# Keys and values one token to a partition, a bias table of single distances, key tiles in the order 0, 3, 1, 2

## The chip, the cores and the metric

The kernel runs on one core of a Trainium2 chip. The metric is the device time of one execution in microseconds, taken as the median of several runs.

## The reference

Attention with a T5-style relative position bias, followed by a mixture of low-rank adapters over the concatenated heads. Batch 8, 8 heads, 576 tokens, head dimension 64; 32 buckets of distance; 8 adapters of rank 16, of which each token uses two.

```python
scores = scale * np.matmul(q, k.transpose(0, 1, 3, 2))        # (8, 8, 576, 576)
n = np.abs(pos[:, None] - pos[None, :])
bucket = np.where(n < 16, n, min(16 + int(log-ratio * 15), 31))   # 31 from n = 128 on
scores = scores + bias_table[bucket].transpose(2, 0, 1)[None]
attn = softmax(scores)
x = (attn @ v), heads side by side                               # (4608, 512)
logits = x @ w_gate                                               # 8 adapters
out = x + sum over the two largest logits of w * ((x @ A[e]) @ B[e])
```

The bias of a query and a key depends on their distance alone, and all distances from 128 on share one bucket. Softmax does not change when that bucket's value is taken off everywhere, so only the band of distances below 128 needs a bias.

## The kernel before, in words

The work is cut into 32 units: one batch and one pair of heads (`units`, 8 x 4). A unit's 576 tokens are 512 "main" tokens and a tail of 64. The tails of all heads of a batch are loaded and cast together (`load_tail`, `cast_tail`).

**Loads.** `load` (L102 to L113) issues the DMAs of a unit's q, k and v from the SP queue: one DMA of 256 KB for q (L112) and, for k and for v, one of 128 KB for each head (L109). Only the two DMAs of the first unit's k are issued from ScalarE's queue. q puts four consecutive tokens on a partition (runs of 1 KB in DRAM). k and v are in two halves of 256 tokens, two consecutive tokens on a partition (runs of 512 B). So key tile c = 2g + e holds the tokens 256 g + 2 p + e. The staging tiles (`qs`, `ks`, `vs`) have four buffers; the program of unit u issues the loads of unit u + 4. SP also stores the results (`out_dram<-ot`, L310, L332), in program order among the loads.

**Casts and turns.** `cast` copies a staged tile to bf16: q and k at L139, v at L135, on GpSimd in the steady state. In the program of unit u, `prep(u)` casts q and k of unit u + 2, and in some units those of unit u + 3 as well; `prep_late(u)` casts v of unit u + 1. `turn` transposes q and k of unit u + 2 on TensorE (L379), together with tiles of the adapters' part, and VectorE copies the result out of PSUM (L381).

**Scores.** `keys(u, c)` computes a 128 x 512 score tile of both heads. Each has four matmuls of 64 x 64 (`QUADS`: two heads and two halves f of 64 keys). First the scores (L436), 512 columns each; then the bias (L441), which adds a piece of the table `Wt` through the anti-diagonal matrix `anti`, only in the band near the diagonal. `BAND` gives for each half where the band starts, its width n in places and its offset in the table; a place covers the four queries of a partition. Of the widths 64, 96, 96, 64, four times each is streamed: 256 or 384 columns. One exponential on ScalarE (L445) then covers 128 x 1024. The key tiles of a unit are taken in the order `KO`; three of them, then the output steps of the unit before, then the fourth. For the last two units `keys_half` (L454, L461, L465) does the same with tiles split by queries.

**Edges.** `edges(u)` computes the scores between main and tail tokens (L495, L498) and their exponential (L500). Their bias is a factor on the exponentials: `edge_l` on GpSimd (L505, table `EL`) for the tail's keys, `edge_t` on VectorE (L510, table `ET`) for the tail's queries. `corner_scores` does the tail against itself, with the factor `EC`.

**The bias table.** Eight heads' distances are laid out in `gx`, from it the even and odd distances in `gp`; `gp` is written to DRAM (L665) and read back as 64 shifted rows a head (`table`, L208) into `Wt`. `near_rows` takes the exponential of the part near the diagonal (L204, tile `Wn`), and `factors_l` and `factors_t` make `EL`, `EC` and `ET` of it with small matmuls.

**Values and adapters.** `step(u, j)` multiplies the probabilities with v (L524 for the main keys, L532 for the tail's keys, which reads the edge tile `pt`, L541 and L543 for the tail's queries), normalises on VectorE (L563, L564), and does pieces of the adapters' part of earlier batches (L571, L627).

All is scheduled by hand: each engine runs its instructions in program order. The score tiles rotate through three PSUM buffers, which they share with the turns and the edges. The loop over u in program order is: `prep`, `load(u + 4)`, three `keys`, `edge_l`, `edge_t`, `step(u - 1, 0)`, `prep_late`, the fourth `keys`, `turn`, `edges(u + 1)`, `step(u - 1, 1)`.

Of the kernel before, what the change touches and what calls it, by code (L numbers as in the profile page):

```python
# [11 lines left out]
BF16 = mybir.dt.bfloat16  # L12
AX = mybir.AxisListType
ALU = mybir.AluOpType
ACT = mybir.ActivationFunctionType
# [22 lines left out]
def kernel(  # L38
# [11 lines left out]
    nc = tc.nc  # L50
    B, H, S, D = q.shape
# [17 lines left out]
    cp = ctx.enter_context(tc.tile_pool(name="const", bufs=1))  # L69
# [31 lines left out]
    def load(u, names="qkv", eng=nc.sync):  # L101
        b, hp = units[u]  # L102
        for nm in names:
            src = {"q": q, "k": k, "v": v}[nm]
            t = stg.tile([128, 2, 4 * D], FP32, name=f"{nm}s", tag=f"{nm}s")
            heads = src[b, 2 * hp:2 * hp + 2, :SM, :]
            if nm != "q":
                for h in range(2):
                    eng.dma_start(out=t[:, h, :].rearrange("p (g x) -> p g x", g=2),  # L109
                                      in_=heads[h].rearrange("(g p c) d -> p g (c d)", g=2, c=2))  # L110
            else:
                eng.dma_start(out=t, in_=heads.rearrange("h (p c) d -> p h (c d)", c=4))  # L112
            stage[(u, nm)] = t  # L113
# [87 lines left out]
    Wn = cp.tile([128, 2, HP, 68], BF16, tag="Wn")  # L201

    def near_rows(i):
        nc.scalar.activation(Wn[:, i].rearrange("p g (x two) -> p g x two", two=2),  # L204
                             _ap(Wt, 128 - 64 * i, [[WN + 1, HP], [1, 34], [GP, 2]]), ACT.Exp, scale=scale)

    def table(h):
        nc.sync.dma_start(out=Wt[h * 64:h * 64 + 64, :, :WN],  # L208
                          in_=_dram(gd, 2 * h * GP, [[1, 64], [4 * GP, HP], [1, WN]]))

    def table_row(rows, hp, y):
        i = 0 if y >= 256 else 1
        return Wn[rows, i, hp, y - 256 + 128 * i:y - 192 + 128 * i]

    def turned(h):
        return anti[h * 64:h * 64 + 64, 64 - 64 * h:128 - 64 * h]

    def factors_l():
        n = HP * 64
        ps = [mp.tile([128, 512], FP32, name="fl", tag="mm") for _ in range(2)]  # L220
        for hp in range(HP):
            for e in range(2):
                for h in range(2):
                    rows = slice(h * 64, h * 64 + 64)
                    for f in range(2):
                        nc.tensor.matmul(ps[h][f * 64:f * 64 + 64, hp * 64 + e * 32:hp * 64 + e * 32 + 32],
                                         lhsT=table_row(rows, hp, 258 - e),
                                         rhs=_ap(turned(h), f, [[2, 32]]),
                                         start=(hp == 0 and e == 0), stop=True, skip_group_check=True)
                    nc.tensor.matmul(_ap(ps[h][rows], n + hp * 64 + e, [[2, 32]]),  # L230
                                     lhsT=table_row(rows, hp, 130 - e), rhs=turned(h)[:, :32],
                                     start=False, stop=True, skip_group_check=True)
        for h in range(2):
            rows = slice(h * 64, h * 64 + 64)
            nc.vector.tensor_copy(EL[:, :, h, :], ps[h][:, :n].rearrange("p (g x) -> p g x", g=HP))
            nc.vector.tensor_copy(EC[rows], ps[h][rows, n:])

    def factors_t():
        ps = [mp.tile([128, 512], FP32, name="ft", tag="mm") for _ in range(2)]
        for hp in range(HP):  # L240
            for e in range(2):
                for h in range(2):
                    rows = slice(h * 64, h * 64 + 64)
                    o = (2 * hp + e) * 64
                    nc.tensor.matmul(ps[h][64:, o:o + 64], lhsT=turned(h), rhs=table_row(rows, hp, 258 - e),
                                     start=(hp == 0 and e == 0), stop=True, skip_group_check=True)
        for h in range(2):
            nc.vector.tensor_copy(ET[64:, :, h, :], ps[h][64:].rearrange("p (g x) -> p g x", g=HP))

    def presets():  # L250
        for t in pts:
# [171 lines left out]
    def open_probs(u):  # L423
        probs[u] = ep.tile([128, 4, 2, SM], BF16, name="pk", tag="pk"), pts[u % 3]

    BAND = (((0, 64, 32), (0, 96, 0)), ((32, 96, 0), (64, 64, 0)))
    QUADS = [(slice(h * 64, h * 64 + 64), slice(f * 64, f * 64 + 64), h, f)
             for f in range(2) for h in range(2)]

    def keys(u, c):  # L430
        b, hp = units[u]
        qT, kT = qkT[u][:, 0, :], qkT[u][:, 1, :]
        sc = score_tile("sc")
        g, e = c // 2, c % 2
        for rows, prt, h, f in QUADS:
            nc.tensor.matmul(sc[prt, h, :],  # L436
                             lhsT=kT[rows, c * 128 + f * 64:c * 128 + f * 64 + 64],
                             rhs=qT[rows, :], start=True, stop=False, skip_group_check=True)
        for rows, prt, h, f in QUADS:
            p0, n, y0 = BAND[g][f]  # L440
            nc.tensor.matmul(_ap(sc[prt, h, :], p0, [[256, 2], [128, 2], [1, n]]), lhsT=turned(h),  # L441
                             rhs=_ap(Wt[rows, hp, :], 2 * y0 + (GP if e else 1),
                                     [[1, 2], [1 - GP if e else GP, 2], [2, n]]),
                             start=False, stop=True, skip_group_check=True)
        nc.scalar.activation(probs[u][0][:, c, :, :], sc, ACT.Exp, scale=scale)  # L445

    def keys_half(u, j, m):
        b, hp = units[u]
        qT, kT = qkT[u][:, 0, :], qkT[u][:, 1, :]
        sc = score_tile("sc")  # L450
        for kk in range(2):
            x0 = (m + 2 * kk) * 128
            for rows, prt, h, f in QUADS:
                nc.tensor.matmul(sc[prt, h, kk * 256:kk * 256 + 256],  # L454
                                 lhsT=kT[rows, x0 + f * 64:x0 + f * 64 + 64],
                                 rhs=_ap(qT[rows, :], j * 128, [[256, 2], [1, 128]]), start=(kk == 0),
                                 stop=False, skip_group_check=True)
        for kk in range(2):
            for rows, prt, h, f in QUADS:
                p0, n, y0 = BAND[kk][f]  # L460
                nc.tensor.matmul(_ap(sc[prt, h, :], kk * 256 + p0, [[128, 2], [1, n]]), lhsT=turned(h),  # L461
                                 rhs=_ap(Wt[rows, hp, :],
                                         2 * y0 + (GP + (1 - GP) * j if m else 1 + GP * j), [[1, 2], [2, n]]),
                                 start=False, stop=True, skip_group_check=True)
        nc.scalar.activation(probs[u][0][:, 2 * j + m, :, :], sc, ACT.Exp, scale=scale)  # L465

# [39 lines left out]

    def edge_t(u, eng=nc.vector):
        hp = units[u][1]
        e = _ap(probs[u][1], 64 + 128, [[SM, 2], [1, 128]])
        eng.tensor_tensor(e, e, ET[:, hp], op=ALU.mult)  # L510

    def pk_slice(u, c, h, t):
# [149 lines left out]
    cast_half(0, "k", 0, nc.scalar)  # L662
    cast_half(0, "k", 1, nc.scalar)
    load(2, "q")
    nc.sync.dma_start(out=gd, in_=gp)  # L665
    cast(0, "q", nc.vector)
    cast_tail(0, "qk", nc.vector, 0, 2)
    load(2, "k")
# [151 lines left out]
    for u in range(2, NU - 2):  # L820
        b, hp = units[u]
# [263 lines left out]
```

## Time and profile before

| what | us |
|---|---|
| median of 3 runs | 190.26 (189.04 to 190.35) |
| the profiled execution | 189.71 |
| its span, first to last instruction of the program | 187.9 |
| ScalarE busy | 163.8 |
| VectorE busy | 136.5 |
| GpSimd busy | 113.3 |

The profile is that of one execution. PE is TensorE's matmuls, PEld its weight loads, DVE VectorE, ACT ScalarE, POOL GpSimd, SP the engine that only issues DMAs; SPq is its queue. A row of a group ends with the busy time, the mean ns of one instruction, and the idle time before them with what ended it. A row of the timeline or of the chain begins with the start and the duration in us. The TensorE clock granted was 0.998 of full speed over the span, so it plays no part here.

### The profile page before, as it was taken

To read this page: it belongs to the slowest core of one execution; us is meant where nothing else is said; L and a number is where in the kernel's file an instruction comes from. 1 tells how busy PE (TensorE), PEld (TensorE's weight loads), DVE (VectorE), ACT (ScalarE), POOL (GpSimd) and SP (SyncE) were. 2 spreads that over 40 slices of the span, in tenths; PEclk is the share of its full clock that TensorE was granted. 3 is DMA by queue.
4 is the path that set the end of the run, shared out by engine and by line. 5 is a ranking of instruction groups with operands and counts; after the bars stand their busy time and mean duration, and the time that the engine had idled before them with its cause. 6 is when DMAs were issued, how large, how long until landed. Compare 5 with 4: busy or idle time off the path is not lost.

```text
span 187.9 us, 9941 instructions
## 1 busy us (share of the span) xinstructions
PE 176.9 (94%) x4293; PEld 126.9 (68%) x4293; DVE 136.5 (73%) x344; ACT 163.8 (87%) x199; POOL 113.3 (60%) x250
## 2 busy tenths in 40 slices
PE   7796899999999999999999999999999999999980
PEld 2344666767777677776777777767777677788940
DVE  7535765586756786888887797779778888788770
ACT  3339999899999999999999999998999989987880
POOL 7453966469279844985298538953486848435230
PEclk9999999999999999999999999999999999999999
DMA  5889998898897877788887975777877874333346
GB/s 143 245 187 252 270 219 227 225 236 241 200 272 219 226 227 221 223 242 206 265 236 216 232 226 151 241 229 204 233 227 217 249 208 115 114 119 107 121 164 229
DMA packets 63668, 39.40 MB, mean 210 GB/s; under 512 B 17409, under 2 KB 58889, under 8 KB 63625
## 3 DMA queue, kind: packets, MB, share of 16 engines
q1 hardware_dynamic: 63000, 38.38, 71.2%
q8 instruction: 33, 0.54, 1.4%
q10 hardware_dynamic: 624, 0.39, 0.8%
q14 instruction: 11, 0.08, 0.2%
HBM read 29.31 MB, written 9.45 MB: 206 GB/s over the span
## 4 chain that ended last, share of the span: by engine, by line
PE 74%; ACT 9%; SPq 5%; DMA 4%; issue 2%; DVE 2%; POOL 1%; ACTq 0%; POOLq 0%
PE pv L524 15%; PE sc L436 14%; ACT pk L445 8%; PE tx L379 7%; PE sc L441 7%; PE dl L627 5%; PE sc L498 4%; PE pv L571 3%; PE pv L541 3%; PE pv L532 3%; PE sc L495 3%; DMA vs<-in_v_dram 2%; DMA ks<-in_k_dram 2%; SPq L109 2%; PE busy L659 2%
## 5 line engine op out<-in xcount | busy, mean ns | idle before, releaser
L445 ACT ACTIVATE pk<-sc 128x1024 bf16<-128x1024 f32 x120 | 113.1, 1030 | 6.2 <-PE sc L441 5.6
L436 PE MATMUL sc<-tx 64*64 64x512 bf16 x480 | 47.1, 388 | 0.7 <-ACT pt L500 0.5
L524 PEld LDWEIGHTS <-pk 128*128 128x128 bf16 x1024 | 37.6, 97 | 9.2 <-issue 2.1
L524 PE MATMUL pv<-v,pk 128*128 128x65 bf16 x992 | 41.3, 193 | 0.0
L441 PE MATMUL sc<-Wt,anti 64*64 64x256 bf16 (+1 forms) x480 | 41.3, 306 | 0.0
L381 DVE COPY tx<-tx 128x2048 bf16<-128x2048 bf16 (+7 forms) x34 | 34.9, 1026 | 4.8 <-PE tx L379 4.0
L500 ACT ACTIVATE pt<-sc 128x1024 bf16<-128x1024 f32 x32 | 33.4, 1044 | 3.2 <-PE sc L498 2.2
L564 DVE TENSOR_TENSOR xn<-pv,rc 128x320 bf16<-128x320 f32 x62 | 30.5, 492 | 2.1
L563 DVE RECIPROCAL rc<-pv 128x5 f32<-128x5 f32 x62 | 12.0, 194 | 19.2 <-PE pv L571 12.3
L505 POOL TENSOR_TENSOR pt<-pt,EL 128x128 bf16<-128x128 bf16 x32 | 13.8, 430 | 19.1 <-ACT pt L500 11.6
L436 PEld LDWEIGHTS <-tx 64*64 64x64 bf16 x480 | 16.4, 104 | 10.7 <-issue 1.8
L304 DVE TENSOR_TENSOR ot<-dl,xn 128x512 f32<-128x512 f32 x25 | 17.2, 689 | 8.5 <-PE dl L627 8.5
L135 POOL CAST v<-vs 128x512 bf16<-128x512 f32 x32 | 20.9, 654 | 4.0 <-PE pv L543 2.2
L139 POOL CAST kn<-ks 128x512 bf16<-128x512 f32 x29 | 18.0, 620 | 3.3 <-DMA ks<-in_k_dram 3.2
L139 POOL CAST qn<-qs 128x512 bf16<-128x512 f32 x30 | 18.9, 631 | 1.3 <-DMA qs<-in_q_dram 1.0
L541 PE MATMUL pv<-v,pt 128*128 128x65 bf16 x248 | 17.8, 194 | 0.0
L532 PE MATMUL pv<-vb,pt 128*128 128x130 bf16 x124 | 17.4, 223 | 0.0
L484 POOL TENSOR_TENSOR pc<-pcx,EC 128x256 bf16<-128x256 bf16 x8 | 5.6, 705 | 18.8 <-ACT pcx L386 16.2
L441 PEld LDWEIGHTS <-anti 64*64 64x64 bf16 x480 | 16.1, 106 | 0.3 <-issue 0.2
L541 PEld LDWEIGHTS <-pt 128*128 128x128 bf16 x256 | 14.0, 98 | 0.1
L510 DVE TENSOR_TENSOR pt<-pt,ET 128x256 bf16<-128x256 bf16 x32 | 13.1, 413 | 0.3
L379 PEld LDWEIGHTS <-qn 64*128 64x128 bf16 x256 | 5.7, 95 | 10.5 <-issue 5.4
(151 smaller groups left out, 293.1 us busy)
## 6 DMA issues: line engine op xcount, KB each, us to landing
qs<-in_q_dram SPq DMA_DIRECT2D x32, 256.0 KB, 4.7
vs<-in_v_dram SPq DMA_DIRECT2D x64, 128.0 KB, 4.2
out_dram<-ot SPq DMA_DIRECT2D x32, 256.0 KB, 3.3
ks<-in_k_dram SPq DMA_DIRECT2D x62, 128.0 KB, 4.4
vt<-in_v_dram SPq DMA_DIRECT2D x8, 128.0 KB, 4.5
qkt<-in_q_dram SPq DMA_DIRECT2D x7, 128.0 KB, 4.8
qkt<-in_k_dram SPq DMA_DIRECT2D x7, 128.0 KB, 3.9
out_dram<-ot SPq DMA_DIRECT2D x7, 128.0 KB, 2.9
```

Source lines behind the costliest of these rows:

```text
L135: eng.tensor_copy(t[:, :, :, :D].rearrange("p c h d -> p h c d"), s)
L139: copy(t.rearrange("p c h d -> p h c d"), s)
L379: nc.tensor.transpose(ps[:, a, cols], src(i, a), ident[rows, rows])
L381: copy(sb[:, :n], ps.rearrange("p a (c i) -> p c a i", i=64)[:, :n])
L436: nc.tensor.matmul(sc[prt, h, :], lhsT=kT[rows, c * 128 + f * 64:c * 128 + f * 64 + 64], rhs=qT[rows, :], start=True, stop=False, skip_gro ...
L441: nc.tensor.matmul(_ap(sc[prt, h, :], p0, [[256, 2], [128, 2], [1, n]]), lhsT=turned(h), rhs=_ap(Wt[rows, hp, :], 2 * y0 + (GP if e else 1 ...
L445: nc.scalar.activation(probs[u][0][:, c, :, :], sc, ACT.Exp, scale=scale)
L500: nc.scalar.activation(probs[u][1][:, 64:], sc.rearrange("p h x -> p (h x)"), ACT.Exp, scale=scale)
L524: nc.tensor.matmul(pv[:, o:o + W1], lhsT=pk_slice(u, c, h, j + 2 * f), rhs=vm[:, c, h, :], start=first, stop=False, skip_group_check=True)
L532: nc.tensor.matmul(_ap(pv, h * W1, [[130, 2], [1, W1]]), lhsT=probs[u][1][:, x0:x0 + 128], rhs=tvs[b % 2][:, 2 * hp + h].rearrange("p f d ...
L541: nc.tensor.matmul(pv[:, o:o + W1], lhsT=probs[u][1][:, x0:x0 + 128], rhs=vts[u % NV][:, c, h, :], start=False, stop=False, skip_group_che ...
L564: nc.vector.tensor_tensor(xs[b][:, j, hp], _ap(pv, 0, [[W1, 5], [1, D]]), _ap(rc, 6 * j, [[1, 5], [0, D]]), op=ALU.mult)
```

## The change

k and v are loaded with one token to a partition in four blocks of 128: key tile c holds the tokens 128 c to 128 c + 127, and a DMA has four runs of 256 B to a partition in place of two of 512 B. The cast, the turn and the value matmuls stay as they are. With that the keys of one half lie 64 next to each other, and the table needs no even and odd parts: `gp` goes, `gx` is mirrored in place and written to DRAM, `Wt` has 320 columns in place of 449, and the bias operand reads it in steps of four in place of two. `BAND` has one entry for each of the eight halves. `ET` covers only the last key tile (all 128 partitions, 64 columns a head) in place of the last two (64 partitions of 128 columns). `KO` is (0, 3, 1, 2) in place of (0, 2, 1, 3).

```diff
-    KO = (0, 2, 1, 3)
+    KO = (0, 3, 1, 2)
...
                 for h in range(2):
-                    eng.dma_start(out=t[:, h, :].rearrange("p (g x) -> p g x", g=2),
-                                      in_=heads[h].rearrange("(g p c) d -> p g (c d)", g=2, c=2))
+                    eng.dma_start(out=t[:, h, :].rearrange("p (c d) -> p c d", c=4),
+                                  in_=heads[h].rearrange("(c p) d -> p c d", c=4))
...
-    GL = 520
-    C = 256
-    GP = 256
-    WN = GP + 193
+    GL = 384
+    C = 191
+    WN = 320
+    NB0 = 128
...
-    gp = cp.tile([H, 2, GP], BF16, tag="gp")
-    ET = cp.tile([128, HP, 2, 128], BF16, tag="ET")
-    nc.vector.memset(gp, 0.0)
+    ET = cp.tile([128, HP, 2, 64], BF16, tag="ET")
     nc.vector.memset(tvs[0], 0.0)
-    nc.vector.memset(ET[:64], 1.0)
...
-    HF = FAR // 2
-    nc.vector.tensor_copy(gp[:, :, HF * 2:HF * 3], _ap(gx, C, [[1, 2], [2, HF]]))
-    nc.vector.tensor_copy(_ap(gp, HF * 2 - 1, [[GP, 2], [-1, HF]]), _ap(gx, C + 2, [[-1, 2], [2, HF]]))
-    gd = nc.dram_tensor("g_d", (H, 2 * GP), BF16, kind="Internal").ap()
-    Wt = cp.tile([128, HP, WN + 1], BF16, tag="Wt")
+    nc.vector.tensor_copy(_ap(gx, C - 1, [[-1, FAR - 1]]), gx[:, C + 1:C + FAR])
+    gd = nc.dram_tensor("g_d", (H, GL), BF16, kind="Internal").ap()
+    Wt = cp.tile([128, HP, WN], BF16, tag="Wt")
...
     def table(h):
-        nc.sync.dma_start(out=Wt[h * 64:h * 64 + 64, :, :WN],
-                          in_=_dram(gd, 2 * h * GP, [[1, 64], [4 * GP, HP], [1, WN]]))
+        nc.sync.dma_start(out=Wt[h * 64:h * 64 + 64], in_=_dram(gd, h * GL, [[1, 64], [2 * GL, HP], [1, WN]]))
...
-    BAND = (((0, 64, 32), (0, 96, 0)), ((32, 96, 0), (64, 64, 0)))
+    BAND = [(max(16 * s - 32, 0), min(16 * s + 48, 128) - max(16 * s - 32, 0), 64 * max(2 - s, 0))
+            for s in range(8)]
...
         for rows, prt, h, f in QUADS:
-            p0, n, y0 = BAND[g][f]
-            nc.tensor.matmul(_ap(sc[prt, h, :], p0, [[256, 2], [128, 2], [1, n]]), lhsT=turned(h),
-                             rhs=_ap(Wt[rows, hp, :], 2 * y0 + (GP if e else 1),
-                                     [[1, 2], [1 - GP if e else GP, 2], [2, n]]),
+            p0, n, y0 = BAND[2 * c + f]
+            nc.tensor.matmul(_ap(sc[prt, h, :], p0, [[128, 4], [1, n]]), lhsT=turned(h),
+                             rhs=_ap(Wt[rows, hp, :], y0, [[1, 4], [4, n]]),
                              start=False, stop=True, skip_group_check=True)
...
-        e = _ap(probs[u][1], 64 + 128, [[SM, 2], [1, 128]])
+        e = _ap(probs[u][1], 64 + 192, [[SM, 2], [1, 64]])
         eng.tensor_tensor(e, e, ET[:, hp], op=ALU.mult)
```

`near_rows`, `factors_l`, `factors_t` and `keys_half` are rewritten to the same layout: 40 small matmuls in place of 48 for `EL` and `EC`, 16 as before for `ET`, two exponentials of 512 and 256 columns in place of two of 272.

More of the change, by code (lines that the diff above doesn't have):

```diff
@@ L193 @@
                         bts[:, buckets[lo]:buckets[lo] + 1].to_broadcast((H, d - lo)))
[L194 to L198 removed]
+    nc.vector.tensor_copy(_ap(gx, C - 1, [[-1, FAR - 1]]), gx[:, C + 1:C + FAR])
+    gd = nc.dram_tensor("g_d", (H, GL), BF16, kind="Internal").ap()
+    Wt = cp.tile([128, HP, WN], BF16, tag="Wt")
     EL = cp.tile([128, HP, 2, 64], BF16, tag="EL")
     EC = cp.tile([128, HP * 64], BF16, tag="EC")
[L201 removed]
+    Wn = cp.tile([128, HP, WN - NB0], BF16, tag="Wn")
     def near_rows(i):
[L204 to L205 removed]
+        x0, x1 = ((64, 192), (0, 64))[i]
+        nc.scalar.activation(Wn[:, :, x0:x1], Wt[:, :, NB0 + x0:NB0 + x1], ACT.Exp, scale=scale)
     def table(h):
[L208 to L209 removed]
+        nc.sync.dma_start(out=Wt[h * 64:h * 64 + 64], in_=_dram(gd, h * GL, [[1, 64], [2 * GL, HP], [1, WN]]))
     def table_row(rows, hp, y):
[L212 to L213 removed]
+        return Wn[rows, hp, y - NB0:y - NB0 + 64]
     def turned(h):
@@ L221, in factors_l @@
         for hp in range(HP):
[L222 to L232, printed above, removed]
+            for x in range(2):
+                for f in range(2):
+                    for h in range(2):
+                        nc.tensor.matmul(_ap(ps[h][f * 64:f * 64 + 64], hp * 64 + x * 16, [[32, 2], [1, 16]]),
+                                         lhsT=table_row(slice(h * 64, h * 64 + 64), hp, 256 - 64 * x),
+                                         rhs=_ap(turned(h), 2 * f, [[1, 2], [4, 16]]),
+                                         start=(hp == 0 and x == 0), stop=True, skip_group_check=True)
+            for h in range(2):
+                rows = slice(h * 64, h * 64 + 64)
+                nc.tensor.matmul(ps[h][rows, n + hp * 64:n + hp * 64 + 64], lhsT=turned(h),
+                                 rhs=table_row(rows, hp, 128), start=False, stop=True, skip_group_check=True)
         for h in range(2):
@@ L240, in factors_t @@
         for hp in range(HP):
-            for e in range(2):
+            for f in range(2):
                 for h in range(2):
[L243 to L246, printed above, removed]
+                    nc.tensor.matmul(ps[h][f * 64:f * 64 + 64, hp * 64:hp * 64 + 64], lhsT=turned(h),
+                                     rhs=table_row(slice(h * 64, h * 64 + 64), hp, 256 - 64 * f),
+                                     start=(hp == 0), stop=True, skip_group_check=True)
         for h in range(2):
-            nc.vector.tensor_copy(ET[64:, :, h, :], ps[h][64:].rearrange("p (g x) -> p g x", g=HP))
+            nc.vector.tensor_copy(ET[:, :, h, :], ps[h][:, :HP * 64].rearrange("p (g x) -> p g x", g=HP))
     def presets():
@@ L433, in keys @@
         sc = score_tile("sc")
-        g, e = c // 2, c % 2
         for rows, prt, h, f in QUADS:
@@ L459, in keys_half @@
             for rows, prt, h, f in QUADS:
-                p0, n, y0 = BAND[kk][f]
+                p0, n, y0 = BAND[2 * (m + 2 * kk) + f]
                 nc.tensor.matmul(_ap(sc[prt, h, :], kk * 256 + p0, [[128, 2], [1, n]]), lhsT=turned(h),
-                                 rhs=_ap(Wt[rows, hp, :],
-                                         2 * y0 + (GP + (1 - GP) * j if m else 1 + GP * j), [[1, 2], [2, n]]),
+                                 rhs=_ap(Wt[rows, hp, :], y0 + j, [[2, 2], [4, n]]),
                                  start=False, stop=True, skip_group_check=True)
@@ L664 @@
     load(2, "q")
-    nc.sync.dma_start(out=gd, in_=gp)
+    nc.sync.dma_start(out=gd, in_=gx)
     cast(0, "q", nc.vector)
```

## The prediction

> **What bounds the kernel now.** I read the page first (busy shares, the chain that ended last, the DMA queues), then the chain in order of time for one cycle of the unit loop early and part of one late, then SP's own rows, which issue the loads.
>
> ```profile
> span 187.9 us, 9941 instructions
> ...
> PE 176.9 (94%) x4293; PEld 126.9 (68%) x4293; DVE 136.5 (73%) x344; ACT 163.8 (87%) x199; POOL 113.3 (60%) x250
> ...
> q1 hardware_dynamic: 63000, 38.38, 71.2%
> ...
> PE 74%; ACT 9%; SPq 5%; DMA 4%; issue 2%; DVE 2%; POOL 1%; ACTq 0%; POOLq 0%
> ...
> L510 DVE TENSOR_TENSOR pt<-pt,ET 128x256 bf16<-128x256 bf16 x32 | 13.1, 413 | 0.3
> ```
>
> TensorE is nearly always at work and carries 74% of the chain. But the chain of an early cycle shows that ScalarE is the other half of a loop:
>
> ```profile
> 42.93 0.34 PE sc L436 x4
> 43.27 0.20 PE sc L441 x4
> ...
> 43.55 2.86 ACT pk L445 x3
> ...
> 46.46 0.29 PE sc L495 x8
> ...
> 46.98 0.60 PE pv L524 x16
> ...
> 47.86 0.34 PE sc L436 x4
> ...
> 48.48 2.86 ACT pk L445 x3
> ```
>
> Three exponentials (L445) free the score buffer that the edge scores (L495) take; then PE does half of the values, then the scores (L436) and bias (L441) of the next unit's first key tile, which the next exponential needs. 48.48 less 43.55 is 4.93 us a unit. Of this loop the change can shorten one piece, the bias of the first key tile. Later PE runs without a gap:
>
> ```profile
> 97.61 0.34 PE sc L436 x4
> 97.94 0.18 PE sc L441 x4
> 98.12 0.21 PE sc L436 x4
> 98.34 0.12 PE sc L441 x4
> 98.46 0.22 PE sc L436 x4
> 98.67 0.17 PE sc L441 x4
> 98.85 0.32 PE dl L627
> ```
>
> The reader is to see how a bias block is paid: 512 columns of scores take 0.21 to 0.22 us, 0.42 ns a column, and the bias in between 0.12 or 0.18, by whether the shorter (256) or the longer (384 columns) of its two halves of the array must end before the next score may start.
>
> **The bias on PE.** Each score tile has two halves (f = 0 and 1, 64 keys each), which run side by side; what counts is the longer sum up to the point where all must end. Before: 256 and 384 columns, in turns. After: BAND gives 48, 64, 80, 80, 80, 80, 64, 48 places by four, so the key tiles 0, 3, 1, 2 have (192, 256), (256, 192), (320, 320), (320, 320). Over the three key tiles ahead of L627, f = 1 falls from 384 + 256 + 384 = 1024 to 256 + 192 + 320 = 768, which is 256 columns or 0.107 us; the fourth tile falls from 384 to 320, 0.027 us. Where PE alone is the bound, a unit gains 0.134 us. Where the loop with ScalarE binds, only the first tile's bias counts: 384 to 256, 0.054 us. The two bounds over 29 units are 1.6 and 3.9 us. I take 0.055 a unit, because with that loop at 4.93 PE cannot use more for long.
>
> One price is not in the trace: the bias operand is now read in steps of four bf16 values instead of two. Today's steps of two cost (0.18 - 0.12) / 128 = 0.47 ns a column, as good as the score's steps of one. Bounds: as fast as now, or half as fast, which adds 1088 columns x 0.42 = 0.46 us a unit. I take as fast, the nearest row. On this the Trainium skill (SBUF — State Buffer, section "Door 1: The DMA port swizzle", its note on cachelines) says that reads keep full bandwidth while at least two fall into one 16-byte line; steps of 8 bytes make exactly two. By that rule the price is zero; no run yet shows steps of 8 bytes on PE.
>
> **ET, tables, start.** L510 halves from 256 to 128 elements: at most 0.2 us of VectorE a unit, off the path (DVE is 73% busy and hardly in the chain), taken as 0. The table work of the start (fewer memsets and copies, a narrower table, fewer small matmuls, a larger exponential of it) moves a few tenths either way between 4 and 16 us. It does not add to the sum, since what follows is set by SP's queue, which does not wait for it.
>
> **The loads.** k and v come in runs of 256 B instead of 512 B: 128 DMAs of 256 runs become 512 each, 32,768 runs more. Two prices follow, on the DMA engines and on SP.
>
> ```profile
> 28.00:62.00 34.00, 32.92 (x849) 23.98 (x838) 22.26 (x54) 32.33 (x38) 23.05 (x45) 1.00 0.84 232
> 62.00:112.00 50.00, 50.00 (x1273) 36.75 (x1270) 40.20 (x96) 47.89 (x56) 31.39 (x61) 1.00 0.81 231
> ...
> 151.00:188.00 37.00, 31.23 (x763) 24.43 (x763) 26.27 (x76) 27.99 (x42) 14.73 (x41) 0.99 0.44 145
> ```
>
> The last two columns of these windows are DMA share and GB/s. The engines: in all, queue 1 takes 0.712 x 187.9 x 16 = 2140 us for 63,000 runs and 38.38 MB. The last stage (nearly only stores, 2 KB a run) takes 0.44 x 37 x 16 = 260 us for 145 x 37 = 5.37 MB, some 2,600 runs. Two equations, with a price by run and one by byte, give 6.4 ns a run (an estimate). A unit's 1,024 added runs then take 1024 x 6.4 / 16 = 0.41 us of the 4.93, and the share goes from 0.84 to 0.92 and from 0.81 to 0.89: fuller, not full. The Trainium skill (DMA: Bandwidth & Descriptors, section "Why small descriptors are slow (HBM only)") gives three extra cycles a packet, 11 for 256 B; by it two packets cost 22 where 512 B cost 19, 16% more on k and v. It speaks against the change but, like the rows, does not fill the engines.
>
> SP is worse. It issues all of this in order:
>
> ```profile
> L109 SPq DMA_DIRECT2D ks<-in_k_dram x62: 368/470/2436, 3.7 to 149.5; - x62
> ...
> L121 SPq DMA_DIRECT2D vt<-in_v_dram x8: 595/698/1556, 11.3 to 127.9; - x8
> ...
> ks<-in_k_dram SPq DMA_DIRECT2D x62, 128.0 KB, 4.4
> ...
> 8.80 1.24 SPq L208 DMA_DIRECT2D Wt<-g_d  x2
> ...
> 50.16 0.99 SPq L109 DMA_DIRECT2D ks<-in_k_dram  x2
> ...
> 109.92 0.36 SPq L310 DMA_DIRECT2D out_dram<-ot  x1
> 112.81 1.18 SPq L332 DMA_DIRECT2D out_dram<-ot  x2
> ...
> 117.09 0.66 SPq L310 DMA_DIRECT2D out_dram<-ot  x1
> 117.80 1.52 SPq L112 DMA_DIRECT2D qs<-in_q_dram  x1
> 119.38 0.98 SPq L109 DMA_DIRECT2D ks<-in_k_dram  x2
> 120.45 0.93 SPq L109 DMA_DIRECT2D vs<-in_v_dram  x2
> 121.48 0.41 SPq L310 DMA_DIRECT2D out_dram<-ot  x1
> ```
>
> The first two rows give least, median and longest ns of an issue, the third the us to landing. An issue with two runs to a partition costs 0.47; those with four (Wt, 1.24 for two) or eight (vt, 0.60 at least) cost about 0.62. For four runs I take 0.62, 0.15 more each; the bounds are 0 (it stays 0.47) and 0.23 (vt's median, stalls included). From 8.80 us to 50 us SP issues almost without a break, so this adds up. Up to the keys of unit 11 (50.16) stand 40 loads of k and v behind 8.80 (units 3 to 11 of k, 0 to 10 of v): 40 x 0.15 = 6.0 us late. Who waits:
>
> ```profile
> 55.89 0.61 POOL L139 CAST kn<-ks 128x512 bf16<-128x512 f32 x1
> 56.47 0.42 POOL L505 TENSOR_TENSOR pt<-pt,EL 128x128 bf16<-128x128 bf16 x1
> ...
> 59.40 0.28 PE L532 MATMUL pv<-vb,pt 128*128 128x130 bf16 x2
> ...
> 136.81 0.62 POOL L139 CAST kn<-ks 128x512 bf16<-128x512 f32 x1 [0.25 <-DMA ks<-in_k_dram]
> 137.38 0.43 POOL L505 TENSOR_TENSOR pt<-pt,EL 128x128 bf16<-128x128 bf16 x1
> ...
> 140.06 0.28 PE L532 MATMUL pv<-vb,pt 128*128 128x130 bf16 x2
> ```
>
> GpSimd casts unit 11's keys at 55.89, nearly as they land. Behind that cast in its queue stands the edge factor of unit 8 (L505, done 56.89), which PE needs at 59.40. Cover: 2.5 us, and 0.8 between landing and cast (an estimate: 50.16, half of the pair's 0.99, and 4.4 to landing make 55.1). So 6.0 - 3.3 = 2.7 us reach PE.
>
> From there the pace can gain 0.055 a unit: 16 units to the next tight place, unit 27's keys (136.81, already waiting for the DMA), -0.9, leaving 1.8. SP at 112.81 has waited some 2.5 us for a result to store, and that swallows as much of its lateness: 6 becomes 3.5. After it SP is full: 117.09 to 121.89 is 4.8 us for a unit of 4.93, and four more times 0.15 makes 5.4, so it falls back 0.5 a unit, to 5.0 at unit 27. Cover there is 140.06 - 137.81 = 2.25, so PE is 2.75 late, of which 1.8 is there already. The last four units give back 0.2, the split tiles at the end 0.15: +2.4.
>
> The sum: 187.9 span within 189.71 for the profiled execution; 189.7 + 2.4 = 192.1. The median of the runs, 190.26, is 0.55 above it; I go half of that way: 192.4.
>
> **The rivals.**
> - *PE's relief wins.* The issue stays at 0.47, or SP's waits were idle anyway. For it: queue engines at 0.81 have room, PE leads the chain. Against: SP's rows stand end to end. Then 29 units gain 0.055 to 0.134, 1.6 to 3.9; time 189.7 - 2.7 = 187.0, faster. Chance 0.25.
> - *They cancel.* The issue costs 0.10 to 0.13: 40 x 0.13 = 5.2 less 3.3 is 1.9 late, with 0.10 it is 0.7; less 29 x 0.055 = 1.6: 188.8 to 190.0, within 1%. For it: the cover is an estimate. Against: the nearest rows say 0.62. Chance 0.20.
> - *The stalls grow too*, 0.23 an issue: 40 x 0.23 = 9.2 less 3.3 is +5.9: 195.6. The engines at 0.92 in the head speak for it. Chance 0.11.
> - *Steps of four halve the bias read*: +0.46 - 0.13 = 0.33 a unit, 29 units: +9.4, 199. Against it the rows of steps of two. Chance 0.05.
> - *The forecast*, queued loads late at units 11 and 27: 191.5 to 194.5, chance 0.39.
>
> **How the numbers follow.** 1% of 190.26 is 1.9 us, about what a measurement of this kernel can tell from no change. Faster is the first rival, 0.25; within it the second, 0.20; slower the rest, 0.39 + 0.11 + 0.05 = 0.55. The range 187.2 to 196.8 cuts off the lower half of the first rival, 0.10, and the upper part of the last two, 0.09. The forecast's own is 191.5 to 194.5.
>
> **What would show it.** Right: issues of ks and vs near 0.62; L139 and L505 on GpSimd waiting for DMA ks around 40 to 60 and 135 to 150 us; L441 down to 48 to 80 places with the chain's dwell near 0.12 to 0.15; DMA share near 0.9; the cycle at 4.87 where nothing is late. Wrong: issues still at 0.47 (then faster); L441 longer than now for fewer columns (then steps of four cost); no wait for the loads though the issues are dear (then the cover was larger than I counted).

## The result and the profile after

The changed kernel takes 197.04 us (median of 6 runs, 196.09 to 197.61) where the kernel before took 189.35 in runs beside it: a ratio of 1.039, 95% interval 1.035 to 1.043. The profiled execution took 196.09. All medians and ranges below hold every run, while the ratios leave out single runs more than 1.5% above the fastest of the same kernel. The page of the changed kernel:

```profile
span 194.3 us, 9922 instructions
...
PE 184.4 (95%) x4285; PEld 126.4 (65%) x4285; DVE 136.1 (70%) x341; ACT 166.0 (85%) x199; POOL 110.9 (57%) x250
...
q1 hardware_dynamic: 95256, 38.25, 77.7%
...
PE 79%; DMA 6%; SPq 6%; ACT 4%; DVE 1%; issue 1%; POOL 1%; POOLq 0%
...
L433 PE MATMUL sc<-Wt,anti 64*64 64x192 bf16 (+1 forms) x480 | 51.1, 397 | 0.9 <-DMA Wt<-g_d 0.9
```

TensorE is busy 7.5 us longer, though it streams fewer bias columns. The row to look at is the bias, L433 (L441 before): 51.1 us in place of 41.3. The groups of instructions with shapes kept apart show why, first before, then after:

```profile
L441 PE MATMUL sc<-Wt,anti 64*64 64x384 bf16 x240 | 40.4, 334 | 0.0
L441 PE MATMUL sc<-Wt,anti 64*64 64x256 bf16 x240 | 33.9, 277 | 0.0
```

```profile
L433 PE MATMUL sc<-Wt,anti 64*64 64x320 bf16 x240 | 27.2, 439 | 0.0
L433 PE MATMUL sc<-Wt,anti 64*64 64x256 bf16 x120 | 23.1, 384 | 0.0
L433 PE MATMUL sc<-Wt,anti 64*64 64x192 bf16 x120 | 20.2, 328 | 0.9 <-DMA Wt<-g_d 0.9
```

From 192 to 320 columns the mean goes from 328 to 439 ns, 0.87 ns a column. Before, 277 ns for 256 and 334 for 384 made 0.45. A column costs twice as much, so 85% of the columns (a mean of 272 a matmul in place of 320) cost more than all of them did. In the chain, in order of time, one unit of the changed kernel:

```profile
63.81 0.34 PE sc L428 x4
...
68.89 0.34 PE sc L428 x4
69.23 0.23 PE sc L433 x4
69.45 0.22 PE sc L428 x4
69.67 0.17 PE sc L433 x4
69.84 0.22 PE sc L428 x4
70.06 0.28 PE sc L433 x4
70.34 0.32 PE dl L617
...
71.67 0.34 PE sc L428 x4
72.01 0.28 PE sc L433 x4
...
74.10 0.34 PE sc L428 x4
```

and the fourth key tile of a unit before:

```profile
100.18 0.34 PE sc L436 x4
100.52 0.12 PE sc L441 x2
100.64 0.62 PE tx L379 x32
```

The first three bias blocks of a unit take 0.23, 0.17 and 0.28; the prediction's rows of before had 0.18, 0.12 and 0.17, so they cost 0.21 us a unit. The fourth takes 0.28 in place of 0.12, of which shorter pieces behind it give back some 0.08. A unit of unbroken PE work now takes 74.10 - 68.89 = 5.21 us where it took 4.92. The starts of each unit's first exponential show the same for the whole run: from about 65 us on, a plain unit (the interval that most units have) takes 5.20 us in place of 4.93, but from 39 to 54 us, where the loop with ScalarE sets the pace, only 4.99 in place of 4.92. From the first unit's first exponential to that of the 30th it is 150.4 us in place of 144.5, which is 5.9 of the 6.4 us that the span has grown.

The loads did get dearer, as these windows (PE busy first, DMA share and GB/s last) and SP's issues show. The waits for them are mixed:

```profile
28.00:62.00 34.00, 33.47 (x813) 23.12 (x807) 20.90 (x53) 31.51 (x36) 22.59 (x44) 1.00 0.96 223
62.00:112.00 50.00, 50.00 (x1232) 34.95 (x1224) 38.89 (x92) 46.44 (x53) 31.32 (x63) 1.00 0.89 226
```

```profile
L109 SPq DMA_DIRECT2D ks<-in_k_dram x62: 367/507/1643, 3.7 to 152.2; - x62
```

```profile
POOL qkb L147 <- DMA qkt<-in_k_dram: 7.1, 4, 3.7
...
POOL kn L139 <- DMA ks<-in_k_dram: 1.2, 2, 0.9
```

The DMA engines are busier than before (0.96 for 0.84) and move less (223 GB/s for 232), but PE hardly stops for it: 33.47 us of 34, where before had 32.92. GpSimd waits 7.1 us for the tails in place of 5.3, and 1.2 for the keys in place of 3.2.

### The profile page after: what moved, and what is told of

It reads as the page before. It is cut to its first block, busy times and chain, and to the rows that moved or that the text cites. A ratio compares the mean times of both kernels' runs of the same rounds, so it can differ in the third digit from the quotient of the medians.

```text
span 194.3 us, 9922 instructions
## 1 busy us (share of the span) xinstructions
PE 184.4 (95%) x4285; PEld 126.4 (65%) x4285; DVE 136.1 (70%) x341; ACT 166.0 (85%) x199; POOL 110.9 (57%) x250
## 3 DMA queue, kind: packets, MB, share of 16 engines
q1 hardware_dynamic: 95256, 38.25, 77.7%
## 4 chain that ended last, share of the span: by engine, by line
PE 79%; DMA 6%; SPq 6%; ACT 4%; DVE 1%; issue 1%; POOL 1%; POOLq 0%
PE pv L514 16%; PE sc L428 15%; PE sc L433 13%; PE tx L371 7%; PE dl L617 5%; PE pv L561 4%; PE pv L531 4%; PE pv L522 3%; PE sc L488 3%; ACT pk L436 3%; DMA Wt<-g_d 2%; PE sc L485 2%; DMA vs<-in_v_dram 2%; DMA g_d<-gx 2%; SPq L109 2%; SPq L127 2%
## 5 line engine op out<-in xcount | busy, mean ns | idle before, releaser
L433 PE MATMUL sc<-Wt,anti 64*64 64x192 bf16 (+1 forms) x480 | 51.1, 397 | 0.9 <-DMA Wt<-g_d 0.9
L428 PE MATMUL sc<-tx 64*64 64x512 bf16 x480 | 49.8, 396 | 0.6 <-ACT pt L490 0.3
L514 PE MATMUL pv<-v,pk 128*128 128x65 bf16 x992 | 41.3, 193 | 0.0
L490 ACT ACTIVATE pt<-sc 128x1024 bf16<-128x1024 f32 x32 | 32.9, 1027 | 3.3 <-PE sc L488 2.2
L135 POOL CAST v<-vs 128x512 bf16<-128x512 f32 x32 | 20.2, 631 | 5.9 <-PE pv L533 2.7
L433 PEld LDWEIGHTS <-anti 64*64 64x64 bf16 x480 | 16.9, 115 | 3.2 <-issue 1.3
L561 PE MATMUL pv<-AW,tx 128*128 128x136 bf16 x124 | 12.5, 224 | 0.0
```

The costliest lines, as they stand in the source:

```text
L135: eng.tensor_copy(t[:, :, :, :D].rearrange("p c h d -> p h c d"), s)
L428: nc.tensor.matmul(sc[prt, h, :], lhsT=kT[rows, c * 128 + f * 64:c * 128 + f * 64 + 64], rhs=qT[rows, :], start=True, stop=False, skip_gro ...
L433: nc.tensor.matmul(_ap(sc[prt, h, :], p0, [[128, 4], [1, n]]), lhsT=turned(h), rhs=_ap(Wt[rows, hp, :], y0, [[1, 4], [4, n]]), start=False ...
L490: nc.scalar.activation(probs[u][1][:, 64:], sc.rearrange("p h x -> p (h x)"), ACT.Exp, scale=scale)
L514: nc.tensor.matmul(pv[:, o:o + W1], lhsT=pk_slice(u, c, h, j + 2 * f), rhs=vm[:, c, h, :], start=first, stop=False, skip_group_check=True)
L561: nc.tensor.matmul(pv[:, o:o + ER + E], lhsT=t.xT[c], rhs=AW[:, c, :], start=first and c == cs[0], stop=(c == HP - 1), skip_group_check=True)
```

## The experiments

Ratios are against the kernel before, run on the same chip beside each. Two explanations stood against each other at first: the bias read in steps of four (S), and the loads in 256-byte runs (L).

**The step alone taken away** (e1).

```diff
-                             rhs=_ap(Wt[rows, hp, :], y0, [[1, 4], [4, n]]),
+                             rhs=_ap(Wt[rows, hp, :], y0, [[1, 4], [1, n]]),
```

> The changed kernel with one thing altered: the bias matmuls (L433, L452) read the table in steps of one value in place of four (same columns, same count; the bias values are then not those of the reference). Theory S (the step of four halves the bias read, 0.87 ns a column against 0.45): the bias blocks go back to about 277 ns for 256 columns and 305 for 320, the unit falls from 5.1 to about 4.87, and the time falls to 186.5 to 189.5 us, at or below the kernel before. Theory L (the loads in runs of 256 B are late): the unit stays as long as in the changed kernel, 195 us or more. If both take part, 190 to 194.

Measured: 192.46 (191.56 to 194.19), ratio 1.014 (1.007 to 1.022). More than half of the loss is gone, not all of it.

**The loads alone put into the kernel before** (e2).

```diff
-                    eng.dma_start(out=t[:, h, :].rearrange("p (g x) -> p g x", g=2),
-                                      in_=heads[h].rearrange("(g p c) d -> p g (c d)", g=2, c=2))
+                    eng.dma_start(out=t[:, h, :].rearrange("p (c d) -> p c d", c=4),
+                                  in_=heads[h].rearrange("(c p) d -> p c d", c=4))
```

> The kernel before with one part of the change alone: k and v are loaded one token to a partition in four blocks (runs of 256 B); everything else is as before, so the order of the keys no longer fits the bias. Theory S: issues of k and v at 0.50 to 0.52 us in place of 0.47, DMA share up by about 0.08, and the time within 1% of before, 188.5 to 191 us. Theory L: 193 us or more, with GpSimd and TensorE waiting for the keys.

Measured: 196.64 (194.57 to 198.22), ratio 1.030 (1.022 to 1.038). The loads by themselves cost nearly as much as the whole change. Where they do it, in the windows:

```profile
28.00:62.00 34.00, 28.95 (x733) 20.88 (x724) 18.89 (x47) 28.29 (x32) 19.73 (x37) 1.00 0.96 213
```

PE works 28.95 us of these 34, 4 us less than before. GpSimd's timeline shows the longest of the stalls, and the same cast before:

```profile
53.24 0.62 POOL L135 CAST v<-vs 128x512 bf16<-128x512 f32 x1
58.16 0.61 POOL L147 CAST qkb<-qkt 128x512 bf16<-128x512 f32 x1 [4.31 <-DMA qkt<-in_k_dram]
...
61.59 0.43 POOL L505 TENSOR_TENSOR pt<-pt,EL 128x128 bf16<-128x128 bf16 x1
```

```profile
52.08 0.62 POOL L147 CAST qkb<-qkt 128x512 bf16<-128x512 f32 x1 [2.52 <-DMA qkt<-in_k_dram]
```

The cast of the tails waits 4.31 us for its transfer in place of 2.52 and runs 6.1 us later, and behind it in the queue stands the edge factor L505, which the prediction's row had at 56.47: it is 5.1 us later.

**A price list for steps** (e4): the bias operand is read from a tile of zeros, in another step in each of eight kinds of unit (the bias values are left out). One execution was taken, for its rows; it took 203.63 us.

```diff
-                             rhs=_ap(Wt[rows, hp, :], y0, [[1, 4], [4, n]]),
+            if u % 8 == 0:   rhs=_ap(Wz[rows, :], y0, [[1, 4], [1, n]])
+            elif u % 8 == 1: rhs=_ap(Wz[rows, :], y0, [[1, 4], [2, n]])
...              # then steps 3, 4, 5, 6, 8, 16
```

> A look at the disputed cost itself: in the changed kernel the bias matmuls read from a tile of zeros in steps of 1, 2, 3, 4, 5, 6, 8 and 16 bf16 values, by the unit (u modulo 8), each on its own line, so the bias is left out. Lengths are 192, 256 and 320 columns as in the changed kernel. Theory S with a line of 16 bytes and a fixed cost a line: 1 and 2 near 0.45 ns a column, 3 somewhat more or the same, 4 near 0.87, 5 to 8 about 1.1 to 1.7, 16 no more than 8. A rule by which two reads a line are enough would have 4 still at 0.45 and the cost only from 5 on. Theory L says nothing of it: all alike.

The groups of 320 columns, costliest first (L439 is step 1, L441 2, L443 3, L445 4, L447 5, L449 6, L451 8, L453 16):

```profile
L449 PE MATMUL sc<-Wz,anti 64*64 64x320 bf16 x32 | 4.7, 579 | 0.0
...
L453 PE MATMUL sc<-Wz,anti 64*64 64x320 bf16 x24 | 4.4, 730 | 0.0
L451 PE MATMUL sc<-Wz,anti 64*64 64x320 bf16 x24 | 4.4, 718 | 0.0
...
L447 PE MATMUL sc<-Wz,anti 64*64 64x320 bf16 x32 | 4.2, 509 | 0.0
...
L445 PE MATMUL sc<-Wz,anti 64*64 64x320 bf16 x32 | 3.6, 439 | 0.0
...
L443 PE MATMUL sc<-Wz,anti 64*64 64x320 bf16 x32 | 3.1, 372 | 0.0
...
L439 PE MATMUL sc<-Wz,anti 64*64 64x320 bf16 x32 | 2.6, 298 | 0.0
L441 PE MATMUL sc<-Wz,anti 64*64 64x320 bf16 x32 | 2.6, 305 | 0.0
```

Steps one and two cost the same within 7 ns; from there each step more adds some 67 to 70 ns to 320 columns, up to step eight; sixteen is no dearer than eight. Step four on a tile of zeros has exactly the 439 ns of the changed kernel, so neither the table nor its values matter. The step does, as theory S had it.

**The two by two completed.** With the 512-byte loads back in the changed kernel, the step of four is what is left beside the columns (e3); with the step taken away as well, the columns alone (e10).

```diff
 # e3: the changed kernel
-                    eng.dma_start(out=t[:, h, :].rearrange("p (c d) -> p c d", c=4),
-                                  in_=heads[h].rearrange("(c p) d -> p c d", c=4))
+                    eng.dma_start(out=t[:, h, :].rearrange("p (g x) -> p g x", g=2),
+                                      in_=heads[h].rearrange("(g p c) d -> p g (c d)", g=2, c=2))
 # e10: the same, and
-                             rhs=_ap(Wt[rows, hp, :], y0, [[1, 4], [4, n]]),
+                             rhs=_ap(Wt[rows, hp, :], y0, [[1, 4], [1, n]]),
```

> The changed kernel with the 512-byte k and v loads of the kernel before, so that what is left of the change is the fewer bias columns in a step of four and the key order (each score tile then gets the bias of other tokens: the work is the same, the values are not). Theory L, the loads' cost is hidden under the slow bias reads in the changed kernel: 195 to 198, the time of the changed kernel, POOL waits on k and q loads gone. Theory A, loads and step of four add up: 191 to 193.5. Measured so far beside 190.4 for the kernel before: 192.5 with the step of four alone taken away, 196.6 with the loads alone put in.

> The changed kernel with the 512-byte loads of the kernel before and the bias read in step one (bias values of other distances in the score tiles): what is left of the change is fewer bias columns and the key order. Theory P, the bound is PE's work and both costs of the change are the two that were taken out: 186.5 to 188.8, one half to two per cent under the kernel before, by 0.055 to 0.134 us a unit. Theory W, a wait takes the place (q and k tails from the DMA, ScalarE's exponentials): 189 to 191. Were there a third cost in the change (order of the key tiles, the tables at the start), it would be over 191.

| bias read | loads of 512 B | loads of 256 B |
|---|---|---|
| before: steps of two, more columns | 1 | 1.030 (1.022 to 1.038), e2 |
| fewer columns, step one | 0.981 (0.976 to 0.987), e10 | 1.014 (1.007 to 1.022), e1 |
| fewer columns, steps of four | 1.033 (1.030 to 1.037), e3 | 1.039 (1.035 to 1.043), the change |

In us: e3 196.51 and e10 187.62, beside 190.12. Fewer columns gain 1.9%, as theory P wanted. Steps of four cost 1.033 / 0.981 = 5.3% with the small loads' cost absent. The loads cost 3.0 to 3.4% where PE is fast (first two rows) and 0.6%, with intervals that overlap, where PE is slow: theory L of e3. The reading is that a TensorE that needs 5.2 us a unit gives the transfers the time that they lack; no run tested this by itself. e3 and e10 ran on one chip, e1 and e2 on another, each beside the kernel before. The bias row of e10:

```profile
L433 PE MATMUL sc<-Wt,anti 64*64 64x192 bf16 (+1 forms) x480 | 35.7, 278 | 0.0
```

35.7 us, 15.4 less than in the changed kernel with the same columns. A plain unit takes 4.86 us.

**How do the loads cost it?** Either SP needs longer to issue them (the prediction's step), or the DMA engines are full and hold up everything in SP's queue. Three kernels on that. First, twice the issues with the same runs (e5):

```diff
 # the kernel before; each k and v transfer in two
+                    for g in range(2):
+                        eng.dma_start(out=t[:, h, 2 * D * g:2 * D * (g + 1)],
+                                      in_=heads[h, 256 * g:256 * (g + 1)].rearrange("(p c) d -> p (c d)", c=2))
```

> The kernel before with each k and v transfer issued as two, one for each half of the keys: the same 512-byte runs and bytes, but 252 issues in place of 126, so more of SyncE's time and none of the DMA engines'. Theory S, the issue on SyncE is what makes the loads late (the prediction's step): at 0.37 us an issue, the shortest in the profile, it is 8 x 0.37 = 2.96 us a unit in place of 4 x 0.47 = 1.88, seven times what the 256-byte runs added (4 x 0.035), so 196 or more. Theory E, the DMA engines' time for the runs is: 189 to 192.5, as before, with SyncE busier and the keys still in time.

Measured: 235.19, ratio 1.234 (1.227 to 1.241). SP's rows, and the window:

```profile
L110 SPq DMA_DIRECT2D vs<-in_v_dram x128: 328/430/1907, 11.3 to 201.1; - x128
L110 SPq DMA_DIRECT2D ks<-in_k_dram x124: 328/431/2447, 3.7 to 199.2; - x124
```

```profile
28.00:62.00 34.00, 26.79 (x590) 19.39 (x584) 15.55 (x36) 22.12 (x24) 15.84 (x30) 0.90 0.59 158
```

Summed over the trace, SP spends 126.4 us on the issues of k and v in place of 71.4, and 45 of these 55 us are in the result: SP's queue has little room for so much. The DMA engines are at 0.59 here, so it is not they that hold it up (the granted clock is lower as well, 0.90 in this window). That is theory S's outcome. But the 256-byte runs add only 0.035 us to the median k or v issue, 4.4 us in all 126. Summed over the trace, all of SP's issues take 150.7 us with the loads alone in place of 135.1, and only 1.4 of the 15.6 us added are on k and v themselves. So a second look was needed: the length of the q issues, which the 256-byte loads don't touch, from 28 to 62 us. Before, and the loads alone:

```profile
L112 SPq DMA_DIRECT2D qs<-in_q_dram x9: 417/469/624, 28.0 to 59.5; - x9
```

```profile
L112 SPq DMA_DIRECT2D qs<-in_q_dram x8: 567/759/1727, 30.7 to 61.5; - x8
```

The same q transfer takes 0.76 us to issue instead of 0.47 (the medians in 28 to 62 us). So it does in e1, while e10, which differs from e1 in the loads alone, has 0.47. Second, the small runs with lighter DMA engines (e6):

```diff
 # the kernel with the loads alone
-                eng.dma_start(out=t, in_=heads.rearrange("h (p c) d -> p h (c d)", c=4))
+                eng.dma_start(out=t[:, :, :D],
+                              in_=heads.rearrange("h (p c) d -> p h c d", c=4)[:, :, 0])
...
+            s = s[:, :, 0:1].to_broadcast((128, 2, 4, D))     # in the cast of q
```

> The kernel before with the 256-byte k and v loads, and of each q load only one token of a partition's four read, which the cast then spreads over all four (the scores are of fewer queries; every later step is the same work). The k and v issues stay as they are with the loads alone (median 0.505 us each), while the DMA engines get back 256 runs x (two runs of 28 ns less one of 18.5) / 16 = 0.6 us a unit, about what the 256-byte runs added (0.66). Theory E, the DMA engines are full and every issue on SyncE is held up behind them: 189.5 to 192.5, the q issue back from 0.76 to about 0.45 us in 28 to 62 us. Theory S, the k and v issues' own length is the cost: 195 to 198, as with the loads alone.

Measured: 189.62, ratio 0.996 (0.993 to 0.999). The q issues, and the page's queue 1:

```profile
L112 SPq DMA_DIRECT2D qs<-in_q_dram x9: 505/510/757, 27.6 to 60.6; - x9
```

```profile
q1 hardware_dynamic: 95256, 32.09, 70.1%
```

All 95,256 runs are still there, and k's issue still takes 0.507; with fewer bytes the share goes to 70.1% and the whole loss is gone, though each k and v issue is still 0.037 us longer in the median: SP does have room for a few us. Theory E holds: the small runs fill the DMA engines, the issues in SP's queue grow with that, and late transfers (the tails' first) stop the casts. One end is open: e2 and e6 ran on different chips, each beside the kernel before. Third, still longer runs in the kernel before (e9):

```diff
+                    eng.dma_start(out=t[:, h, :], in_=heads[h].rearrange("(p c) d -> p (c d)", c=4))
```

> The kernel before with k and v read in 1024-byte runs, four tokens to a partition in one block (keys are then scored against the bias of other tokens: the work is the same, the values are not). Theory E, the DMA engines' time for the runs sets how early loads land: half the runs of the kernel before, its engine share over 28 to 62 us falls from 0.84 to some 0.75, and the time to 186.5 to 188.8. Theory S or a kernel whose PE covers its loads already: 189 to 191, no change.

Measured: 190.33, ratio 1.000 (0.996 to 1.003). Theory E's number was missed, and so was its premise:

```profile
q1 hardware_dynamic: 46872, 38.38, 70.0%
...
28.00:62.00 34.00, 31.71 (x801) 23.06 (x802) 21.02 (x52) 31.04 (x36) 21.37 (x42) 1.00 0.80 224
```

The share falls to 0.80 and not to 0.75, and over the span from 71.2% to 70.0%. The DMA records of the traces, one for each run that an engine moved, say why: a run of 1024 bytes takes an engine 55.2 ns on average, and two of 512 take 2 x 28.3, so longer runs give it hardly less work. This run therefore says little of what lighter engines would bring. As to where the cost sets in: e10 doesn't pay it at an engine share of 0.87 in this window, and e1, with the small runs, pays it at 0.92. The share alone doesn't decide it, since the changed kernel stands at 0.96 and loses 0.6%.

**The order of the key tiles** (g1): the changed kernel with `KO = (0, 2, 1, 3)`.

> The changed kernel with the key tiles in the order of the kernel before (0, 2, 1, 3). Theory: the order of the tiles costs nothing, since each tile has the same number of bias columns over its four quarters but for the first and last: 196 to 198, as the changed kernel. Rival: the wide tiles 1 and 2 at the unit's end are what ScalarE waits for: 194 to 195.5.

Measured: 198.47, ratio 1.044 (1.041 to 1.046). That is just above the theory's range of 196 to 198. The new order is not a cost; if anything it is worth half a per cent, though the intervals just overlap.

**Mending the change.** The table copied once into four planes, so that the whole computation runs with step one (f1, and in more rounds f1b):

```diff
+            e.tensor_copy(Wp[:, 2 * i:2 * i + 2], Wt[:, 2 * i:2 * i + 2].rearrange("p g (i r) -> p g r i", r=4))
...
-                             rhs=_ap(Wt[rows, hp, :], y0, [[1, 4], [4, n]]),
+                             rhs=_ap(Wp[rows, hp], y0 // 4, [[WN // 4, 4], [1, n]]),
```

> The changed kernel with the table copied once, after it has landed, into four planes (Wp[.., j, i] = Wt[.., 4 i + j], half on VectorE and half on GpSimd), which the bias matmuls then read in steps of one. The result is the reference's. Theory S: 0.7 to 1.3 us later at the start, then units of 4.87 us: 187 to 190 us, with luck faster than the kernel before (189.4). Theory L: 195 us or more, as the loads are untouched.

> The changed kernel with the bias table copied once on chip into four planes, so that every bias read is in step one, in more rounds than the first time (194.0, with runs from 190.2 to 196.8). It does the whole computation. Theory E: what is left is the columns' gain of about 1.9 per cent and the 256-byte loads' loss of 3 to 3.4, so 191.5 to 194, 0.7 to 2 per cent slower than before, with the q issue in 28 to 62 us still near 0.6 to 0.76 us. Rival: the planes' two copies at the start also cost, 1 to 2 us more: 194 to 196.

Measured: 194.01 (190.16 to 196.78, too scattered for a ratio) beside 190.41, which neither theory of f1 had, then on another chip 190.67 (189.28 to 193.62, 12 runs) beside 189.26, ratio 1.004 (1.000 to 1.007). The second time it is better than expected, level with the kernel before and not ahead of it. Its q issues from 28 to 62 us are still long, and the engines full:

```profile
L112 SPq DMA_DIRECT2D qs<-in_q_dram x8: 452/624/1518, 29.0 to 58.8; - x8
```

```profile
28.00:62.00 34.00, 30.30 (x748) 21.93 (x744) 20.06 (x48) 29.28 (x34) 21.25 (x43) 0.95 0.96 219
```

So in the second set of runs the gain of the columns and the loss by the loads cancel, with the loads at some 2.3% (1.004 / 0.981) and not 3.0 to 3.4. Why e1, which does less, and the first runs of this kernel came out slower, both on the same chip, was not tried. Last, the planes with k in 1024-byte runs, its tokens put in order by VectorE's copy after the turn (f3):

```diff
+                for h in range(2):
+                    eng.dma_start(out=t[:, h, :], in_=heads[h].rearrange("(p c) d -> p (c d)", c=4))
...
+            copy(sb[:, x + 4:x + 8].rearrange("p c a i -> p (c a i)").rearrange("p (a i c) -> p a c i", a=2, c=4),
+                 ps[:, :, (x + 4) * 64:(x + 8) * 64].rearrange("p a (c i) -> p a c i", c=4))
```

> The changed kernel with both costs attacked: the bias table is copied once into four planes so that it is read in step one, and k is read in 1024-byte runs, its tokens put in order by the copy after the transpose (one DVE copy of 128x2048 becomes two or three, with writes 8 bytes apart), so that only v has 256-byte runs. Theory E and the sum: half of the loads' 4.9 us is back, from 192.5 to 190 and the planes' copies 0 to 1.5 on top: 189.5 to 191.5. Rival, the split copies on DVE lie on the way from the transposes to the scores and cost 0.1 to 0.4 us in each of 32 units: 193 to 202.

Measured: 203.32, ratio 1.069 (1.066 to 1.073). The rival named the cause, and its range of 193 to 202 was still too low:

```profile
L386 DVE COPY tx<-tx 128x512 bf16<-128x512 bf16 x32 | 41.6, 1301 | 0.0
...
L385 DVE COPY tx<-tx 128x512 bf16<-128x512 bf16 x32 | 13.5, 421 | 4.5 <-PE tx L379 4.2
```

The copy that puts the tokens in order takes 1301 ns, the same size in order 421, on the way from the turn to the scores; VectorE has 44% of the chain of this run. No version here that computes the reference's result beats the kernel before.

## Why the prediction was wrong, point by point

- *What bounds the kernel* was right: PE, with ScalarE close behind.
- *PE's relief*, 0.055 to 0.134 us a unit, was right: e10's 187.62 is 2.5 us under 190.12, 0.09 a unit over 29, and a plain unit there takes 4.86 us in place of 4.93 (it reads in steps of one, 0.42 ns a column for 0.45).
- *"I take as fast, the nearest row"* is the step that failed. The price of a step of four was set at zero, its other bound at half the speed. The trace has 0.87 ns a column for 0.45, almost exactly the half, and e3 shows it with the old loads: +6.3 us (0.033 x 190.12), the gain of the columns already taken off; against e10, which differs in the step alone, it is 8.9 us. Steps of one and two, both free, were taken as a trend, though two points on a flat part say nothing of where it ends. The rival that named this had a chance of 0.05; its 199 was 2 us above the result, since it counted +0.33 us in each of 29 units, where e3 shows 6.3 / 29 = 0.22: a plain unit of the changed kernel is 0.27 longer late in the run and only 0.07 early, where the loop with ScalarE binds. The Trainium skill (SBUF — State Buffer, section "Door 1: The DMA port swizzle", its note on cachelines) gives full bandwidth from two reads in a 16-byte line on. The measurement decides otherwise for this operand: steps of two, four reads in a line, are the last that are free, and steps of four, two reads in a line, halve the rate.
- *The engines, "fuller, not full"*: the shares came as forecast or a little above (0.96 and 0.89 for 0.92 and 0.89), but the price of a run, 6.4 ns, was too low. With the loads alone queue 1 takes 0.797 x 194.3 x 16 = 2478 us, 337 more than before for 32,256 added runs: 10.4 ns. The DMA records of the kernel before had a nearer price: 18.7 ns on average for 256 bytes and 28.3 for 512, so two runs for one add 9. And 0.92 was read as room, where e1 already pays at that share. The estimate of 16% more on k and v by the cycles that the Trainium skill gives (DMA: Bandwidth & Descriptors, section "Why small descriptors are slow (HBM only)") was low as well: by the prediction's two prices 512 bytes cost 29.6 ns, and 10.4 on top is a third more, an estimate; by the records it is 37.4 for 28.3, a third as well.
- *SP, "for four runs I take 0.62"*: the median issue is 0.507, 0.037 more and not 0.15. The 6.0 us of lateness at unit 11's keys was nearly met all the same, by luck, with the loads alone:

```profile
55.85 1.03 SPq L109 DMA_DIRECT2D ks<-in_k_dram  x2
```

  That is 5.7 us after the 50.16 of before, but 40 x 0.037 gives only 1.5 of it; for the rest there are the longer issues behind full engines, as in the q rows above; a share for each was not measured. That SP's queue passes its time on was right, and e5 shows it to an extent that the prediction didn't claim.
- *The cover of 3.3 us* was counted at the cast of unit 11's keys. What stopped GpSimd longest with the loads alone was the tails' transfer, whose cast stands five places earlier in its queue, and little of the delay was absorbed (+5.6 us in e2, 0.030 x 190.41).
- *Units 11 and 27 late* did not happen in the changed kernel: waits for ks are 1.2 us in all. The slow bias read made the loads' cost all but vanish, which no case of the prediction combined. Its forecast of a small loss came from the loads; the measured loss comes from the step. That it pointed to a loss at all was luck.
- *ET* was right to be left out: L500 takes 381 ns where L510 took 413.

## What to carry to other kernels

Before changing the layout of an operand that TensorE streams, work out how many elements it takes from each 16 bytes; a step that is free says nothing of the next one, so measure that step alone before taking fewer columns for a gain. Where one queue issues all loads and is always busy, look at the length of an issue that the change doesn't touch: if it grows together with the share of the DMA engines, as here, it is their work and not the number of issues that must fall. And two costs that sit on different engines need not add; take both out one by one and together, since the smaller is hidden as long as the larger is there.

## What the runs showed of the hardware that was not expected

- TensorE's moving operand in bf16 costs 0.42, 0.45, 0.66, 0.87, 1.08, 1.30, 1.73 and 1.77 ns a column in steps of 1, 2, 3, 4, 5, 6, 8 and 16 (means of 192 and 320 columns, 128 apart, in matmuls on 64x64 quarters of the array): flat up to two, then in proportion to the step up to eight, where each column has 16 bytes to itself.
- A run of 256 bytes takes a DMA engine 18.7 ns, one of 512 takes 28.3 and one of 1024 takes 55 to 57 (means of the traces' records, before and e9): halving 512 bytes costs a third more, doubling them saves nothing to speak of.
- An issue on SP takes longer while the DMA engines are at 0.96 (0.76 us for 0.47, the same transfer), and the same bytes in runs half as long move at 213 GB/s with the engines at 0.96, where they moved at 232 with 0.84.
- Splitting 126 transfers into 252 with the same runs cost 45 us, 0.36 us for each issue added, with the DMA engines at 0.59.
- VectorE's copy of 128x512 bf16 out of PSUM takes 421 ns in order and 1301 with its writes 8 bytes apart.
